# The first two steps of a recurrent attention and PReLU network, cut into named pieces and put in a new order

## The chip, the cores and the metric

The kernel runs on one core of a Trainium2 chip. The metric is the device time of one execution in microseconds; lower is better. The core's engines are TensorE (PE; PEld is its weight load), VectorE (DVE), ScalarE (ACT), GpSimd (POOL) and SyncE (SP). They run side by side, each takes its own instructions strictly in the order in which the program put them, and semaphores make one wait for another.

## What is computed

```python
# q, k, v, f_logit: (batch 4, heads 8, seq 768, head_dim 48), all float32
f = 1 / (1 + exp(-f_logit))
for t in range(S):
    state = f[:, :, t, :, None] * state + einsum('bhd,bhe->bhde', k[:, :, t], v[:, :, t])
    y[:, :, t] = einsum('bhd,bhde->bhe', q[:, :, t], state)
x = y.transpose(0, 2, 1, 3).reshape(3072, 384)      # tokens x (heads * head_dim)
h = x @ w_in                                        # 384 -> 2048
g = maximum(h, 0) + alpha * minimum(h, 0)
out = g @ w_out                                     # 2048 -> 384
```

A gated linear recurrence (a state of 48x48 per head that decays by f and takes in an outer product of k and v at each token), and behind it a network of two layers on each token.

## The kernel before

**Steps.** The sequence is cut into 6 chunks of 128 tokens, the batch into 2 pairs. A step is one chunk of one pair: 12 steps, `(bp, c)`, the pair changing fastest. So steps 0 and 1 are the first chunks of both pairs (c = 0), which have no state before them and take a form of their own for part of the work.

**Layout.** Head dimension lies on partitions, two heads in one tile (rows 0 to 47 and 64 to 111). A chunk has halves of 64 tokens (`CH`) and blocks of 32 (`DB`), a block 8 groups of 4 (`NB`).

**A step's stages** are Python generators; each `yield` ends a piece:

- `prepare` (P): loads of f, q, k and v (L266, L276; SyncE's queue in step 0, GpSimd's else). ScalarE makes the sigmoid and copies q to `qd` (L279, L282); VectorE makes products of neighbouring gates (`kr`) and queries lagged by 1 to 3 tokens (L287). Then two scans that give products of gates from a half's start and to its end (`ps`, `ss`, L317, L319), the query times its gate (`q4` within `us`, L321), the key times gates up to its group's end (`k4`, L347), and from these factors for groups further apart (`near`, L344, for c = 0; `earlier`, L330, else), keys carried to a block's or a half's end (`kh`, `ks`, `ended`, L374, L398), queries from a half's start (`q3`, `started`, L368, L406). For c = 0 it makes `k16` and `q16` (L387, L404), the two sides of the products between the two 16-token halves of a block. Last, ScalarE copies q3 into the matrix `A` (L419).
- `carry` (O): `across` (L476) makes the scores between the two blocks of a half and, for c = 0, the half-block products one block at a time (L486: 64 products of 32x16, both into the tile `off`), from where ScalarE copies them to `ad` (L490) and `A` (L494). For c = 0 `ks` is turned on TensorE (`pk`, L507) and copied to `ksn` (L510). `increments` (L460) makes the state's increments `pd`, `moved` (L443 to L449) the new state, kept in rows of `vs`.
- `attend` (S): for each of the two batches u, the scores of tokens up to 3 apart (`raw`, L532: k against the lagged queries), put where they belong by four masked copies (L538, `ad`), then the scores of groups further apart (`qu`, L548: k4 against us) with masked copies of their own (L570 for c = 0, L554 else). `ad` is copied into `A` (L576), `py` is A times `vs` (L587): 64 columns of values and state at once, and the step's output y is copied out (L596). In step 0 the tokens' layout for the network, `xT`, is made by products with a constant `dense` (L605) and copied (L607); in other steps by DMA (L616).
- `network` (n): 8 pieces `ph` (L631, x times w_in, two tiles of 128 features each), for each of which ScalarE makes `neg` (L636) and VectorE two `gate` (L638). Then the second product. Step 0 does it in full (`po`, L651); the other steps use 7 products of half size instead of 8 (`pa` to `pe`, L670, with sums of VectorE at L674 and L715).

**Weights.** They come in 8 pieces each for w_in and w_out: a load by SyncE and two conversions by ScalarE (L220 to L225; pieces `a` for w_in, `b` for w_out), and an add by VectorE (L234; pieces `w` and `v`). A load's buffer (5 of them) is free when ScalarE has converted it. `W` makes sums of quarters of w_out (L734).

**Order.** TensorE, VectorE and ScalarE take their instructions exactly in the order that `ORDER` gives; GpSimd's and SyncE's are put in order by what they wait for. `FIRST` lists the pieces around steps 0 to 3, `USUAL` all steps behind:

```python
FIRST = (
        "P5 a2 P a O w S w a w a2 S Q S O S w Q2 S Q2 S w",
        "a2 w2 n O b w n b2 S P v2 n2 S b v Q n b n O S2 v n b v n Q2 b v Q b n S v2 W Q W S n2 W n",
```

A letter stands for the next piece of that stage, a number for how often, `Q` for `P` of the step behind. The loop at the end calls `next(...)` on each.

**PSUM.** 8 banks: two pairs (`pair`: raw, qu, off, pk, pd, py take turns in two slots of two banks) and four single banks (`bank`: xt, ph, po, pa to pe). Before the first piece TensorE runs 56 tiny products (`IDLE`, L749).

Of the kernel before, what the change touches and what calls it, by code (L numbers as in the profile page):

```python
# [17 lines left out]
C = 128  # L18
# [12 lines left out]
FIRST = (  # L31
        "P5 a2 P a O w S w a w a2 S Q S O S w Q2 S Q2 S w",
        "a2 w2 n O b w n b2 S P v2 n2 S b v Q n b n O S2 v n b v n Q2 b v Q b n S v2 W Q W S n2 W n",
        "n S P n2 S W n W n Q n3 O S Q n S Q n Q S2 Q n3",
        "S n3 P S Q S n2 O n4 Q S Q S Q n S Q n Q n2",
# [3 lines left out]
def flat(first, usual, steps=12):  # L39
    out = []  # L40
    left = {}
    for n in range(steps + 1):
        for key in (first[n] if n < len(first) else usual).split():
            for _ in range(int(key[1:] or 1)):
                k = key[0]
                if k in "awbvW":
                    out.append((k,))
                else:
                    m = n - 1 if k == "n" else n + 1 if k == "Q" else n
                    k = "P" if k == "Q" else k  # L50
                    if 0 <= m < steps:
                        out.append((k, m))
    return out

ORDER = flat(FIRST, USUAL)


@with_exitstack
def kernel(
# [198 lines left out]
    def prepare(bp, c, x):  # L258
# [5 lines left out]
        def load(name, src, bufs=2):  # L264
            t = work.tile([128, W], F32, tag=name, name=f"{name}_{i}", bufs=bufs)
            loads.dma_start(out=t.rearrange("p (u x) -> p u x", u=U),  # L266
                              in_=src[b0:b0 + U, c].rearrange("u p h t -> p u (h t)"))
            return t

        f = quads(load("f", fT, 1))  # L270
        q = load("q", qT, 1)
        k = x["k"] = load("k", kT, 1)

# [4 lines left out]

        nc.scalar.activation(f, f, AF.Sigmoid)  # L279
        nc.scalar.copy(kr[:, :, 2:3], f[:, :, 3:4])  # L280
        qdv = [qd[:, :, QO[d]:QO[d] + NB * (4 - d)].rearrange("p g (i r) -> p g i r", r=4 - d) for d in range(4)]
        nc.scalar.copy(qd[:, :, 0:DB], q.rearrange("p (g t) -> p g t", t=DB))  # L282
        fq = fs[:, 0:NS - 1].rearrange("p (g i) -> p g i", i=NB + 1)[:, :, 1:NB + 1]
# [12 lines left out]
        yield  # L296

        ps = work.tile([128, NS], F32, tag="ps", name=f"ps_{i}", bufs=1)  # L300
        ut = work.tile([128, G * UW], F32, tag="us", name=f"us_{i}", bufs=1)
        if c:
            us = ut.rearrange("p (g t) -> p g t", g=G)
        else:

            at = (0, VW, VW + 16, VW + 16 + DB, VW + 16 + DB + NB)
            us, q16, k16, g16 = (ut[:, G * lo:G * hi].rearrange("p (g t) -> p g t", g=G) for lo, hi in zip(at, at[1:]))
            nc.gpsimd.memset(k16[:, :, 16:DB], 0.0)
            nc.gpsimd.memset(g16[:, :, 3:5], 1.0)
            x["q16"], x["k16"] = q16, k16  # L310
        x["us"] = us
        q4 = us[:, :, 0:DB].rearrange("p g (i r) -> p g i r", r=4)
        for r in range(4):
            nc.scalar.copy(q4[:, :, :, r], qdv[r][:, :, :, 0])
        if not c:
            nc.scalar.copy(g16[:, :, 2:6:3], fq[:, :, 3:5])
# [3 lines left out]
        yield  # L320
        nc.vector.tensor_tensor(q4, q4, f[:, :, 0:1].rearrange("p (g i) o -> p g i o", i=NB)  # L321
                                .broadcast_to((128, G, NB, 4)), ALU.mult)
        pre = ps[:, 0:NS - 1].rearrange("p (g i) -> p g i", i=NB + 1)
        suf = ss[:, 1:NS].rearrange("p (g i) -> p g i", i=NB + 1)[:, :, 1:NB + 1]

        def earlier(m):

            n = NB - m
            skip = UO[m - 1] + (8 if m == 2 else 4)
            nc.vector.tensor_tensor(  # L330
                us[:, :, UO[m]:UO[m] + 4 * n].rearrange("p g (i r) -> p g i r", r=4),
                us[:, :, skip:skip + 4 * n].rearrange("p g (i r) -> p g i r", r=4),
                fq[:, :, 1:1 + n].unsqueeze(3).broadcast_to((128, G, n, 4)), ALU.mult)

        def near(m, half=None):

            if m == 2:
                to, of = (us[:, :, o:o + 8].rearrange("p g (i r) -> p g i r", r=4) for o in (VO[2] + 8 * half, 16 * half + 8))
                by = fq[:, :, NQ * half + 1:NQ * half + 3]
            else:  # L340
                to = us[:, :, VO[3]:VO[3] + 8].rearrange("p g (i r) -> p g i r", r=4)
                of = us[:, :, VO[2]:VO[2] + 16].rearrange("p g (h r) -> p g h r", r=8)[:, :, :, 4:8]
                by = fq[:, :, 1:NB:NQ]
            nc.vector.tensor_tensor(to, of, by.unsqueeze(3).broadcast_to((128, G, 2, 4)), ALU.mult)  # L344

        k4 = x["k4"] = work.tile([128, W], F32, tag="k4", name=f"k4_{i}", bufs=1)
        nc.vector.tensor_tensor(k4, k, kr.rearrange("p n r -> p (n r)"), ALU.mult)  # L347
        if c:
            earlier(2)
        else:  # L350
            nc.vector.tensor_tensor(g16[:, :, 1:7:5], g16[:, :, 2:6:3], fq[:, :, 2:6:3], ALU.mult)
            near(2, 0)
            nc.vector.tensor_tensor(g16[:, :, 0:8:7], g16[:, :, 1:7:5], fq[:, :, 1:7:5], ALU.mult)
        yield


        q3 = x["q3"] = work.tile([128, GC, 3, DB], F32, tag="q3", name=f"q3_{i}", bufs=1)
        ks = x["ks"] = work.tile([128, GC, 2, DB], F32, tag="ks", name=f"ks_{i}", bufs=1)
        kh = x["kh"] = work.tile([128, GC, DB], F32, tag="kh", name=f"kh_{i}", bufs=1)
        f32 = pre[:, :, NB:NB + 1]  # L360

        some = slice(0, GC) if c else slice(1, GC, 2)

        def started(j):
            gs_ = some if j == 0 else slice(0, GC)
            js = slice(2 * (gs_.start or 0) + j, G, 2 * (gs_.step or 1))
            to = q3[:, gs_, 2 * j]
            nc.vector.tensor_tensor(to.rearrange("p g (i r) -> p g i r", r=4), q4[:, js],  # L368
                                    pre[:, js, 0:NB].unsqueeze(3).broadcast_to((128, to.shape[1], NB, 4)), ALU.mult)

        def ended(j):
            js = slice(j, G, 2)
            kj = ks[:, :, 1] if j else kh
            nc.vector.tensor_tensor(kj.rearrange("p g (i r) -> p g i r", r=4),  # L374
                                    k4.rearrange("p (g i r) -> p g i r", i=NB, r=4)[:, js],
                                    suf[:, js].unsqueeze(3).broadcast_to((128, GC, NB, 4)), ALU.mult)

        ended(0)
        if c:
            earlier(3)  # L380
        else:
            near(2, 1)
        ended(1)
        if c:
            earlier(4)
        else:
            nc.vector.tensor_tensor(k16[:, :, 0:16].rearrange("p g (i r) -> p g i r", r=4),  # L387
                                    k4.rearrange("p (g i r) -> p g i r", i=NB, r=4)[:, :, 0:NQ],
                                    g16[:, :, 0:NQ].unsqueeze(3).broadcast_to((128, G, NQ, 4)), ALU.mult)
        started(1)  # L390
        if c:
            earlier(5)
        else:
            near(3)
        yield
        if c:
            earlier(6)
        nc.vector.tensor_tensor(ks[:, :, 0], kh, f32[:, 1:G:2].broadcast_to((128, GC, DB)), ALU.mult)  # L398
        if c:
            kt = x["kt"] = late["kt"].tile([128, W], F32, tag="kt", name=f"kt_{i}")  # L400
            nc.vector.transpose(kt, ks.rearrange("p g s t -> p (g s t)"))
            earlier(7)
        else:
            nc.vector.tensor_tensor(q16.rearrange("p g (i r) -> p g i r", r=4), q4[:, :, NQ:NB], g16[:, :, NQ:NB].unsqueeze(3).broadcast_to((128, G, NQ, 4)), ALU.mult)  # L404
        by = f32[:, 2 * some.start:G:2 * (some.step or 1)]
        nc.vector.tensor_tensor(q3[:, some, 1], q3[:, some, 2], by.broadcast_to((128, by.shape[1], DB)), ALU.mult)  # L406
        started(0)

        f64 = x["f64"] = work.tile([128, U, H], F32, tag="f64", name=f"f64_{i}")
        by64 = pre.rearrange("p (a c j) i -> p a c j i", c=NC2, j=2)  # L410
        for cc in range(0 if c else 1, NC2 if c < NC - 1 else 1):
            for par in range(2):
                g64 = by64[rows(par), :, cc, :, NB]
                nc.vector.tensor_tensor(f64[halves(cc)[1], :, par:H:2].rearrange("p u h -> p (u h)"),
                                        g64[:, :, 0], g64[:, :, 1], ALU.mult)
        yield
        for cc in range(0 if c else 1, NC2):
            for par in range(2):
                nc.scalar.copy(A[halves(cc)[1], :, par * HP:(par + 1) * HP, CH * cc:CH * (cc + 1)],  # L419
                               q3[rows(par)].rearrange("p (u h c) s t -> p u h c (s t)", h=HP, c=NC2)[:, :, :, cc, 0:CH])  # L420
# [391 lines left out]
```

## Time and profile before

| what | value |
|---|---|
| time, median of 3 runs | 615.39 us (615.17 to 615.62) |
| the profiled execution's own time | 614.73 us |
| its span, from first to last instruction | 612.9 us |
| PE busy | 585.0 us (95%), 8220 instructions |
| PEld busy | 525.4 us (86%) |
| DVE busy | 496.7 us (81%), 997 instructions |
| ACT busy | 246.5 us (40%), 466 instructions |
| POOL busy | 62.8 us (10%) |
| mean granted TensorE clock | 0.997 |

How to read it: an engine's busy time is a sum over stages with different limits. The slices of the span, 40 of equal length, show where an engine is full: a digit is the busy share in tenths. The chain of waits names who waited for whom. The timeline has one row for instructions of one line that follow each other, with the idle time before the row in square brackets and what ended it; "issue" is a wait for nothing that the profile shows. A product in float32 leaves two records on PE, so a row's count is twice the number of instructions (not for the turns `pk`).

### The profile page before, as it was taken

The page shows a single profiled execution, that of the slowest core. Times are in us where ns is not written, and L with a number is a line of the kernel's source. Part 1 is how long each engine was busy: PE and PEld are TensorE (multiplying, and loading weights), DVE is VectorE, ACT ScalarE, POOL GpSimd, SP SyncE. Part 2 cuts the span into 40 slices and gives each one's busy share as a digit, 9 for nine tenths or more (in the row PEclk, how much of TensorE's full clock was granted, in tenths as well). Part 3 has the DMA queues.
Part 4 walks back from the last instruction along what each step waited for, and adds up shares of the span by engine and source line. Part 5 has one row for each costly group of instructions (what it writes and reads, how often), then busy time and mean ns, then how long its engine had stood idle before and what let it go on. Part 6 is the DMA issues. An engine that isn't in the chain of part 4 may idle for free.

```text
span 612.9 us, 19072 instructions
## 1 busy us (share of the span) xinstructions
PE 585.0 (95%) x8220; PEld 525.4 (86%) x8220; DVE 496.7 (81%) x997; ACT 246.5 (40%) x466; POOL 62.8 (10%) x117
## 2 busy tenths in 40 slices
PE   4569999999999999999999999999999999999997
PEld 3458867898899899899899899899899889889997
DVE  7599898899899798798798798798898889762251
ACT  5678852351641261272261261362252253232110
POOL 9120010001010011001001001001001000000000
PEclk9999999999999999999999999999999999999999
DMA  8966432104404214314313313313313401201000
GB/s 303 364 227 202 159 87 53 47 28 108 101 18 88 71 39 107 66 37 98 77 35 91 85 36 90 86 36 87 88 36 87 84 7 27 54 2 27 27 0 27
DMA packets 68116, 50.43 MB, mean 82 GB/s; under 512 B 47168, under 2 KB 60608, under 8 KB 68032
## 3 DMA queue, kind: packets, MB, share of 16 engines
q1 hardware_dynamic: 56656, 25.01, 15.7%
q0 software_dynamic: 6864, 22.35, 12.6%
q10 hardware_dynamic: 4512, 1.85, 1.7%
q8 instruction: 65, 1.06, 0.7%
q14 instruction: 19, 0.16, 0.1%
HBM read 36.21 MB, written 4.72 MB: 67 GB/s over the span
## 4 chain that ended last, share of the span: by engine, by line
PE 86%; DVE 9%; ACT 2%; issue 1%; DMA 1%; SPq 0%; ACTq 0%; DVEq 0%
PE ph L631 39%; PE pc L670 9%; PE pa L670 9%; PE pd L670 5%; PE pe L670 4%; PE pb L670 4%; PE py L587 3%; PE po L651 3%; PE raw L532 3%; PE qu L548 3%; PE pd L460 1%; PE off L476 1%; DVE ad L538 1%; DVE qd L287 1%; DVE gate L638 1%
## 5 line engine op out<-in xcount | busy, mean ns | idle before, releaser
L631 PE MATMUL ph<-xT,w_in_sb 128*128 128x256 f32 x1152 | 258.0, 382 | 1.4 <-DVE Csum L674 0.8
L631 PEld LDWEIGHTS ph<-xT,w_in_sb 128*128 128x128 f32 x1152 | 216.3, 190 | 34.0 <-issue 3.2
L636 ACT ACTIVATE neg<-ph 128x512 f32<-128x512 f32 x96 | 57.2, 596 | 189.1 <-PE ph L631 137.3
L638 DVE SCALAR_TENSOR_TENSOR gate<-neg,om,ph 128x256 f32<-128x256 f32 x192 | 82.7, 478 | 47.4 <-ACT neg L636 47.2
L670 PE MATMUL pc<-t,S 128*128 128x192 f32 x352 | 61.7, 329 | 0.0
L670 PE MATMUL pa<-w_out_sb,gate 128*128 128x192 f32 x352 | 61.4, 327 | 0.2 <-DVE gate L638 0.2
L670 PEld LDWEIGHTS pa<-w_out_sb,gate 128*128 128x128 f32 x352 | 57.9, 190 | 1.3 <-DVE gate L638 0.5
L670 PEld LDWEIGHTS pc<-t,S 128*128 128x128 f32 x352 | 57.3, 190 | 0.6
L538 DVE COPY_PREDICATED ad<-mraw,raw 128x256 f32<-128x256 int32 (+1 forms) x96 | 42.4, 442 | 10.7 <-PE raw L532 8.2
L554 DVE COPY_PREDICATED ad<-mquad,qu 128x224 f32<-128x224 int32 (+6 forms) x140 | 41.9, 299 | 6.2
L419 ACT COPY A<-q 48x512 f32<-48x512 f32 x44 | 27.2, 618 | 36.5 <-DVE q L368 36.1
L576 ACT COPY A<-ad 32x256 f32<-32x256 f32 x96 | 38.8, 404 | 1.4
L330 DVE TENSOR_TENSOR us<-us,fs 128x768 f32<-128x768 f32 (+5 forms) x60 | 36.8, 614 | 0.0
L691 ACT ACTIVATE o<-pa 128x192 f32<-128x192 f32 x11 | 3.6, 331 | 75.2 <-PE pa L670 72.3
L674 DVE SCALAR_TENSOR_TENSOR Csum<-pc,Csum 128x192 f32<-128x192 f32 x22 | 7.9, 357 | 29.6 <-PE pc L670 29.3
L715 DVE TENSOR_TENSOR S<-gate 128x512 f32<-128x512 f32 x44 | 30.3, 688 | 0.8
L532 PEld LDWEIGHTS raw<-qd,k 48*32 48x32 f32 x1536 | 18.6, 109 | 14.2 <-issue 12.0
L670 PE MATMUL pe<-w_out_sb,S 128*128 128x192 f32 x176 | 30.4, 326 | 0.0
L670 PE MATMUL pb<-t,gate 128*128 128x192 f32 x176 | 30.4, 326 | 0.0
L670 PE MATMUL pd<-w_out_sb,S 128*128 128x192 f32 x176 | 30.4, 326 | 0.0
L532 PE MATMUL raw<-qd,k 48*32 48x80 f32 x1536 | 24.1, 243 | 6.5 <-issue 3.4
L266 POOL DMA_DIRECT2D k<-in_kT x11 | 8.0, 728 | 207.4 <-PE raw L532 207.4
(101 smaller groups left out, 766.3 us busy)
## 6 DMA issues: line engine op xcount, KB each, us to landing
w_out_raw<-in_w_out SPq DMA_DIRECT2D x8, 767.8 KB, 5.8
w_in_raw<-in_w_in SPq DMA_DIRECT2D x8, 767.2 KB, 10.8
q<-in_qT POOLq DMA_DIRECT2D x11, 512.0 KB, 4.1
f<-in_fT POOLq DMA_DIRECT2D x11, 512.0 KB, 4.3
k<-in_kT POOLq DMA_DIRECT2D x11, 512.0 KB, 5.0
out<-o SPq DMA_DIRECT2D x24, 192.0 KB, 3.1
vs<-in_v POOLq DMA_DIRECT2D x22, 192.0 KB, 4.6
ksn<-kt SPq DMA_DIRECT2D x80, 32.0 KB, 2.0
```

The lines of the kernel that those rows point to most:

```text
L330: nc.vector.tensor_tensor(us[:, :, UO[m]:UO[m] + 4 * n].rearrange("p g (i r) -> p g i r", r=4), us[:, :, skip:skip + 4 * n].rearrange("p g ...
L419: nc.scalar.copy(A[halves(cc)[1], :, par * HP:(par + 1) * HP, CH * cc:CH * (cc + 1)], q3[rows(par)].rearrange("p (u h c) s t -> p u h c (s ...
L532: nc.tensor.matmul(raw[DB * j:DB * (j + 1), par, hp * C:hp * C + QW], lhsT=k[r_, g * DB:(g + 1) * DB], rhs=qd[r_, g], start=True, stop=True)
L538: nc.vector.copy_predicated(adu[:, :, :, d:4], mraw[:, d, :, d:4].bitcast(I32).unsqueeze(1).broadcast_to((128, H, NB, n)), rv[:, :, QO[d]: ...
L548: nc.tensor.matmul(qu[DB * j:DB * (j + 1), par, hp * QS + 4:hp * QS + QL], lhsT=k4[r_, g * DB:(g + 1) * DB], rhs=us[r_, g, 4:QL], start=Tr ...
L554: nc.vector.copy_predicated(ad[:, u, :, :, 4 * m:DB], mquad[:, lo:lo + n].bitcast(I32).unsqueeze(1).unsqueeze(1).broadcast_to((128, 2, HP, ...
L576: nc.scalar.copy(A[s_, u, :, s_], ad[s_, u].rearrange("p r h t -> p (r h) t"))
L631: nc.tensor.matmul(ph[:, j * T:(j + 1) * T], lhsT=w_in_sb[:, kt, m * 128:(m + 1) * 128], rhs=xT[:, kt], start=(kt == 0 and j == 0), stop=( ...
L636: nc.scalar.activation(neg, phv, AF.Relu, scale=-1.0)
L638: nc.vector.scalar_tensor_tensor(gate[:, m % NH, m // NH], neg[:, j], om[:, m:m + 1], phv[:, j], ALU.mult, ALU.add)
L670: nc.tensor.matmul(to[:, 0:DH], lhsT=of(f), rhs=by(f), start=(f == 0 and not more), stop=(f == NH - 1), skip_group_check=True)
L715: nc.vector.tensor_tensor(to, x_, y_, op)
```

## The change

Steps 0 and 1 (c = 0) are no longer run by the three generators. `opening` gives each of their parts a key of its own, a plain function, and `HEAD` lists the parts of both steps, the weight pieces and the network's pieces one by one. A leading 0 or 1 is the step; in the other words the number behind the letter is the step. `prepare`, `carry` and `attend` keep only the form for c > 0; the shared parts are moved into functions (`loaded`, `scanned`, `gated`, `keyed`, `started`, `ended`, `carried`, `begun`, `turned`, `increments`, `moved`, `across`, `crossed`, `scored`, `scored4`, `lags`, `placed`, `summed`, `by_token`) with the same instructions. `USUAL`, the network and the weight pieces are as before.

Within the two steps: `raw` (r) stands directly behind the lagged queries and takes both slots of the pair; the four `q3`, `kh` and `ks` products come before the group factors; the half-block products are made for four blocks at once (L626 there: a product of 128 keys with 64 queries, of which the diagonal squares of 32x16 are used) into the free end of `qu`, and copied out in four pieces of 16 partitions for each batch; in step 0 `off` and `pk` use single banks; `py`, the copy of y and the dense product are pieces by batch (`y`, `Y`, `x`).

```diff
-FIRST = (
-        "P5 a2 P a O w S w a w a2 S Q S O S w Q2 S Q2 S w",
...
+HEAD = (
+        "0f 0r0 0g a 0h 0i 0r1 0m 0j 0o a 0O 0l 0k 0p a 0R0 0K0 0q 0K1 0s 0u0 b 0t 0U0 0u1 0H0 0d 0R1 0U1 1f 0A0 0H1 "
+        "w 0D 0y0 0A1 0y1 0Y0 0Y1 w 0M 0x0 w 0x1 ",
+        "1r1 1g 1h 1r0 0X a 1i w 1j 1R0 a 1R1 w v a n0 b a w n0 1m a 1l n0 v w n0 w b n0 b 1p 1o v 1q b n0 1k 1O n0 b "
+        "v 1K0 1s 1K1 ",
+        "n0 1u1 1u0 n0 1U0 b v 1U1 P2 1H0 1A0 v 1d n0 1H1 b 1t 1D v 1y0 1A1 1y1 v W 1Y0 P2 1Y1 W 1X W W n0 1M P2 P2 "
+        "P2 n0 n1 S2 P2 W n1 n1 n1 n1 ",
+        "S2 S2 P3 n1 P3 n1 n1 O2 P3 S2 n1 n1 S2 P3 P3 n1 S2 n1 n1 S3 n2 P3 n2 S3 n2 n2 P4 n2 S3 S3 n2 O3 n2 n2 S3 S3 "
+        "P4 n2 P4 n2 P4 P4 n2 P4 n2 n2 ",
+)
...
+        def two(name):
+            if bp:
+                t = pair(name)
+                return t[:, 0], t[:, 1]
+            return bank(f"{name}a"), bank(f"{name}b")
...
+        def quads_of_half():
+            g16 = x["g16"]
+            nc.vector.tensor_tensor(g16[:, :, 1:7:5], g16[:, :, 2:6:3], fq[:, :, 2:6:3], ALU.mult)
+            near(2, 0)
+            nc.vector.tensor_tensor(g16[:, :, 0:8:7], g16[:, :, 1:7:5], fq[:, :, 1:7:5], ALU.mult)
+            near(2, 1)
+            near(3)
...
+        def quad_(u):
+            qu = x["qu", u] = pair(f"qu{u}_{i}")
+            scored4(qu, u, x, VW, C)
+            for hp in range(HP):
+                g = (u * HP + hp) * NJ
+                for par in range(2):
+                    r_ = rows(par)
+                    nc.tensor.matmul(qu[:, par, hp * C + 64:(hp + 1) * C], lhsT=x["k16"][r_, g:g + NJ].rearrange("p j t -> p (j t)"),
+                                     rhs=x["q16"][r_, g:g + NJ].rearrange("p j t -> p (j t)"), start=True, stop=True)
+
+        def halved(u):
+            qv = x["qu", u].rearrange("p r (h x) -> p r h x", h=HP)
+            for j in range(NJ):
+                s_ = slice(DB * j, DB * j + 16)
+                nc.scalar.copy(ad[s_, u, :, :, 16:DB], qv[s_, :, :, 64 + 16 * j:80 + 16 * j])
...
+        def out_(u):
+            if not u:
+                x["py"] = pair(f"py_{i}")
+            summed(x["py"], bp, u)
+
+        def kept_out(u):
+            if not u:
+                x["y"] = work.tile([128, U, HP, C], F32, tag="ksn", name=f"y_{i}", bufs=1)
+            nc.scalar.copy(x["y"][:, u].rearrange("p h t -> p (h t)"), x["py"][:, u])
+
+        def dense_(u):
+            if not u:
+                x["xt"] = [bank(f"xt{kt}_{i}") for kt in range(NK)]
+            for kt in range(NK):
+                pairs = [hp for hp in range(HP) if 2 * D * hp < 128 * (kt + 1) and 2 * D * (hp + 1) > 128 * kt]
+                for hp in pairs:
+                    o = 2 * D - 2 * D * hp + 128 * kt
+                    nc.tensor.matmul(x["xt"][kt][:, u * C:(u + 1) * C], lhsT=dense[:, o:o + 128], rhs=x["y"][:, u, hp],
+                                     start=(hp == pairs[0]), stop=(hp == pairs[-1]))
...
+        parts = {
+            "f": lambda: loaded(bp, c, x), "g": lambda: scanned(bp, c, x), "h": lambda: gated(bp, c, x),
+            "i": lambda: keyed(bp, c, x), "j": lambda: ended(0, x), "l": keys, "m": lambda: started(1, x),
+            "p": quads_of_half, "q": halves_of_block, "s": lambda: begun(bp, c, x), "t": lambda: turned(c, x),
+            "o": off_, "O": lambda: crossed(x["off"]), "k": turn, "d": lambda: increments(bp, c, x),
+            "D": lambda: moved(bp, c, x, 0), "M": lambda: moved(bp, c, x, 1), "X": given,
+        }
+        for key, part in (("r", raw_), ("R", lambda u: lags(x["raw", u], u)), ("u", quad_), ("H", halved),
+                          ("U", quartered), ("K", kept_keys), ("A", placed), ("y", out_), ("Y", kept_out), ("x", dense_)):
+            for u in range(U):
+                parts[f"{key}{u}"] = lambda part=part, u=u: part(u)
...
+        for key, n in ORDER:
+            part = pieces[key] if n is None else run[key, n]
+            part() if callable(part) else next(part)
```

`keys` (l) is `ended(1)` and `carried`; `raw_` and `off_` call `scored` and `across`, `turn` makes `pk`, `given` (X) copies the dense products to `xT` in step 0 and starts the DMAs of `by_token` in step 1. `quartered` (U) holds the three masked copies of L570.

## The prediction

> **What bounds the kernel now.** First the page's slices (15.3 us each):
>
> ```profile
> PE   4569999999999999999999999999999999999997
> DVE  7599898899899798798798798798898889762251
> ```
>
> TensorE fills every slice but the first three and the last; VectorE is nearly full until slice 34. So nearly all that can be saved is TensorE's empty time in the opening. Who it waits for there, from the chain of waits over the first 130 us (us in total, times, longest):
>
> ```profile
> PE off L476 <- DVE q L368: 9.5, 1, 9.5
> PE raw L532 <- issue: 3.4, 3, 2.0
> ...
> PE xt L605 <- ACT y L596: 2.0, 1, 2.0
> PE raw L532 <- ACT A L494: 1.8, 1, 1.8
> ...
> PE raw L532 <- DVE ad L538: 1.3, 1, 1.3
> PE pd L460 <- issue: 1.3, 1, 1.3
> ```
>
> Then the timeline of TensorE (start, us, tile, xcount of records, idle before):
>
> ```profile
> 17.70 1.08 PE L476 MATMUL off<-q,kh 48*32 48x32 f32 x64 [9.46 <-DVE q L368]
> ...
> 24.42 1.02 PE L532 MATMUL raw<-qd,k 48*32 48x80 f32 x38 [1.75 <-ACT A L494]
> ...
> 32.32 0.64 PE L532 MATMUL raw<-qd,k 48*32 48x80 f32 x22 [1.99 <-issue]
> ...
> 38.21 3.17 PE L587 MATMUL py<-A,vs 128*64 128x64 f32 x60 [0.64 <-ACT vs L449]
> 43.39 4.51 PE L605 MATMUL xt<-y,dense 128*128 128x256 f32 x12 [2.00 <-ACT y L596]
> 47.74 2.76 PE L631 MATMUL ph<-xT,w_in_sb 128*128 128x256 f32 x12
> ...
> 51.03 1.34 PE L486 MATMUL off<-us 48*32 48x16 f32 x128
> 52.52 1.09 PE L507 MATMUL pk<-ident,ks 128*128 128x128 f32 x8
> ```
>
> The network of step 0 (`ph`) starts at 47.74 us, and from there TensorE works almost without a wait to 612.9: 565.2 us. So the sum is: when does `ph` start, and what does TensorE still have to do then.
>
> A second reading: TensorE runs at half speed in the opening. 38 records of `raw` take 1.02 us (27 ns each) at 24.42, but 64 take 0.92 us at 63.70 (14 ns); the 12 of `xt` take 4.51 us, the 12 of `ph` behind them, of the same shape, 2.76. PEclk's 9s do not show it.
>
> **The change, part by part.** Times are from the span's start.
>
> 1. First scores. `raw0` and `raw1` need only qd and k. The last lagged query ends at 10.54 on VectorE, k landed at 7.8. Cold, each is 64 x 27 ns = 1.72 us: 10.6 to 14.1, in time in which TensorE now waits (9.46 us before `off`). Cost nothing; if that cover were gone, 3.4 us.
>
> 2. VectorE up to k4 is unchanged (starts at 12.95, the next at 14.11). Then four of 128x512 at a 0.60 us pitch (one q3, both ended, carried) to 16.5; five short ones of quads_of_half (0.20+0.33+0.19+0.33+0.33) to 17.9; the four lags of `raw0` (27.30 to 29.28: 1.98) to 19.9, where they stand at 27.3 now; two half-block factors (1.2) to 21.1; begun (0.33+0.34+0.36) to 22.1.
>
> 3. TensorE: `off` at 15.4 (needs kh and q3 only) for 1.08; `pk` to 18.6; `qu0` at 20.0, when lags of `raw0` free its PSUM pair: 64 records at 19 ns (58 in 1.10 at 26.89) and the 8 half-block products after 21.1, to 22.7.
>
> Those products: 128 records of 32x16, 1.34 us a step, become 16 instructions 128 wide and 64 long. Below by py's rows (64 columns, 32 instructions in 2.08: 65 ns): 1.0 us; above by pk's (128x128, 8 in 1.09: 136 ns): 2.2. I take 1.0, since like py they fill two tiles side by side: -0.3 a step.
>
> 4. Copies of those halves go from 2 to 8 a step, as 16-partition pieces of 128 elements. The row before is 0.43 us for 2 of the same length, so 0.8 us for four. They now stand on the path: after quartered(0) (1.00 us, to 23.7) ScalarE copies to 24.5; only that frees the pair that `qu1` takes (the built program has `qu1` wait for ScalarE). `qu1` 24.6 to 27.1, quartered(1) to 28.3, its copies to 29.2.
>
> 5. `pd` 27.1 to 29.0 (1.95), its copies to 30.0 (0.96); `py` to 33.8 (0.48+3.17). "Output by batch" does less than it says: in the built program the first copy of y waits for the last product of both batches. So y is 34.0 to 35.1 (1.07), and only the dense product starts after its first half, 34.6.
>
> 6. `xt` has the columns of before: 2.7 us at full speed, 5.3 at half. ScalarE has step 1's us copies between (2.17+0.32, to 37.6), hidden by it. Then both `raw` of step 1 (1.7 to 3.4) before `ph`. At half speed throughout, `ph` starts at 34.6+5.3+3.4 = 43.2; at full speed from `py` on (`py` then ends at 32.1), at about 37.1. In the trace `py`'s 60 records take 53 ns each, between the 32 of the `py` at 81.92 (64 in 2.08) and twice that, so the clock came up within it, and `xt`, behind a wait of 2.00, is slow again. The new order has no wait over 1 us from `pd` on, so I take 39.8.
>
> [...]
> [...] The rows show `pk` starting at 52.52 right behind 32-wide products that run to 52.37; so I price no drain.
>
> 7. What runs behind `ph`: the two `raw` (0.85 each at full speed) are done: -1.7.
>
> 8. "Issue" waits (0.96, 1.99, 1.30): time in which TensorE waits for nothing shown. They may come back at other places: 0 to 4.3. Some will fall into the waits before `qu0` and `qu1`: +1.5.
>
> 9. VectorE in the first network. From 28.3: step 1's lagged queries 3.65, two w_in adds 1.9, vs 2.0, w_in 1.0, scans, gate and k4 3.6, then a wait for ScalarE's conversion of w_in3, which stands behind xT, to 42; that add, kh, eight lags of step 1 (3.9), two adds: the first gate at about 49.3, ended 50.1. Four `ph` banks fill from 39.8 to 50.6 (2.69 each), so the fifth `ph` has 0.5 us of cover. If it is gone, each us late costs a us. +0.2.
>
> 10. Loads. SP's w_out0 goes ahead of w_in3, and w_in7's load waits until ScalarE converts w_in3 (40): landed 46 to 47, added at about 58, needed at 60 or later: cover 2 us. POOL issues q, f and k of step 1 at once (now k at 33.4).
>
> 11. Steps 2 and 3 have their pieces in another order, with no instruction added. TensorE is full there now (its waits behind 130 us in the profile, `ph` for Csum 0.8 and for issue 0.6, are small), which hides an earlier or later VectorE or DMA step; priced at nothing, 1 us more if a piece comes late.
>
> Sum: -7.9 (39.8 for 47.7) -1.7 -0.3 +1.5 +0.2 = -8.2. On the profiled execution, 614.73 (span 612.9 and 1.8 around it), that is 606.5; the median, 615.39, is 0.66 higher, so the forecast is 607.2. Best ends: -10.6-1.7-0.3+1.0 = -11.6, 603.8. Worst: -4.5-1.7+0.9 (`ph` still cold)+0.5 (products)+4.3 +1.0 = +0.5, 615.9.
>
> **Rivals.**
> A. The clock comes up early and issue waits hide: `ph` at 37.1, about 604. For: few waits from 24.6 on. Against: at 24.4 to 28.0 `raw` and `qu` at 70% duty stayed slow.
> B. VectorE becomes the bound of the first network: gates late by 3 to 6 us, cover 0.5: 610 to 613. For: VectorE is busy 19.7 of the 20 us from 40 to 60 now, and it sheds only the wait of 6.1 and 1.1 at `ad`, where TensorE wants 8. Against: its list above fits.
> C. Slower: ScalarE's queue. Step 1's sigmoid now stands before the copies of A, the second half-block copies, pd's and y. It is reached at 24.5 and needs f's load. In the trace that load was issued by POOL at 15.2 and landed at 23.6 (8.4 us; the median of such loads is 4.3), among weight loads that land every 2.03 us. Each us past 24.5 is a us on the path, and past 32.7 the gain is used up. Six weight loads served first would be 16.9+6x2.03 = 29.1, then q and f; at 35 the time is 617.7. Against: POOL's loads shared the engines with SP's.
>
> **How the numbers follow.** Forecast (605 to 610) 0.53, A 0.16, B 0.18, C 0.10, nothing left (within 0.2%) 0.03. A time within 0.2%, 1.2 us, can't be told from no change. Faster: 0.53+0.16+0.16 of B = 0.85; same 0.04; slower 0.11. The range goes from A to B: 603 to 612.5.
>
> **What would show it.** `raw` at 10.6 and `off` at 15.4; `qu0` near 20, `qu1` near 24.6 behind ScalarE's ad copies; `ph` at 37 to 43; no wait of `ph` for gates over 1 us. It is wrong if sigmoid waits for its DMA past 26, if `ph` waits for `gate`, or if TensorE shows new issue waits over 4 us before `ph`.

## The result, and the profile after

The changed kernel takes 606.56 us (median of 4 runs, 606.23 to 606.95), the kernel before 615.50 beside it: ratio 0.9855, 95% interval 0.9838 to 0.9873. The forecast was 607.2. The profiled execution took 606.23 us, its span is 604.5, so 8.4 us are gone from the span of 612.9.

The slices of the page (tenths busy, 15.1 us each):

```profile
PE   5689999999999999999999999999999999999997
DVE  7799999998898888889889899798798798761351
```

TensorE gains in the first three slices (4, 5 and 6 tenths before) and nowhere else that a tenth shows. Its chain of waits over the whole run (us in total, times, longest):

```profile
PE raw L489 <- DVE qd L289: 2.6, 1, 2.6
PE qu L498 <- ACT ad L633: 2.2, 1, 2.2
...
PE off_0a L463 <- DVE kh L358: 1.7, 1, 1.7
...
PE ph L716 <- issue: 0.9, 1, 0.9
...
PE raw L489 <- issue: 0.8, 2, 0.4
```

The one wait of 9.5 for q is now 2.6 + 1.7 with the first scores between them, and `raw`'s issue waits fell from 3.4 to 0.8. A new one, of `qu` for ScalarE's copies, is 2.2. The timeline of TensorE (start, us, tile, records, idle before):

```profile
10.88 2.12 PE L489 MATMUL raw<-qd,k 48*32 48x80 f32 x111 [2.64 <-DVE qd L289]
13.40 0.60 PE L489 MATMUL raw<-qd,k 48*32 48x80 f32 x17 [0.40 <-issue]
...
20.49 1.05 PE L498 MATMUL qu<-us,k 48*32 48x52 f32 x64 [1.54 <-DVE ad L506]
21.60 1.97 PE L626 MATMUL qu<-us 48*128 48x64 f32 x16
25.81 1.06 PE L498 MATMUL qu<-us,k 48*32 48x52 f32 x64 [2.23 <-ACT ad L633]
...
28.70 1.53 PE L436 MATMUL pd<-vs,ksn 64*48 64x48 f32 x64
31.18 0.48 PE L521 MATMUL py<-A,vs 128*64 128x64 f32 x4 [0.95 <-ACT ad L633]
...
36.02 2.92 PE L683 MATMUL xt<-y,dense 128*128 128x128 f32 x24 [0.78 <-ACT y L674]
...
40.65 0.47 PE L489 MATMUL raw<-qd,k 48*32 48x80 f32 x21 [0.38 <-issue]
41.05 13.22 PE L716 MATMUL ph<-xT,w_in_sb 128*128 128x256 f32 x60
```

`ph` starts at 41.05 for 47.74: 6.69 us earlier. Behind it stand 604.5 - 41.05 = 563.45 us for 565.2: 1.75 less. Together that is the 8.4. `xt` took 2.92 us, so TensorE's clock was up before it: the record of the granted clock has it at full from 34.66.

One line each from ScalarE's and VectorE's timelines, for the two queues that the rivals named:

```profile
25.78 1.06 ACT L283 ACTIVATE f<-f 128x1024 f32<-128x1024 f32 x1
```

```profile
49.29 0.86 DVE L723 SCALAR_TENSOR_TENSOR gate<-neg,om,ph 128x256 f32<-128x256 f32 x2
```

Step 1's sigmoid ran without a wait (f had landed at 24.26), and the first gate is at 49.29, as forecast, with no wait of `ph` behind it.

### The profile page after: what moved, and what is told of

The parts are those of the page before. It is cut to its first block, busy times and chain, and to the rows that moved or that the text cites. A ratio compares the mean times of both kernels' runs of the same rounds, so it can differ in the third digit from the quotient of the medians.

```text
span 604.5 us, 18724 instructions
## 1 busy us (share of the span) xinstructions
PE 585.7 (97%) x8040; PEld 526.9 (87%) x8040; DVE 495.7 (82%) x997; ACT 249.5 (41%) x478; POOL 62.8 (10%) x117
## 3 DMA queue, kind: packets, MB, share of 16 engines
q0 software_dynamic: 6864, 22.35, 13.1%
q8 instruction: 64, 1.05, 0.8%
## 4 chain that ended last, share of the span: by engine, by line
PE 90%; DVE 4%; ACT 2%; DMA 2%; SPq 1%; issue 1%; DVEq 0%; ACTq 0%
PE ph L716 40%; PE pc L755 9%; PE pa L755 9%; PE pb L755 5%; PE pe L755 4%; PE pd L755 4%; PE py L521 4%; PE po L736 4%; PE qu L498 3%; PE raw L489 3%; PE pd L436 2%; PE off L463 1%; SPq L422 1%; DMA ksn<-kt 1%; DMA f<-in_fT 1%
## 5 line engine op out<-in xcount | busy, mean ns | idle before, releaser
L325 ACT COPY us<-qd 128x256 f32<-128x256 f32 x48 | 27.0, 672 | 7.4 <-DVE qd L289 4.4
L289 DVE TENSOR_TENSOR qd<-qd,f 128x768 f32<-128x768 f32 (+2 forms) x36 | 27.1, 752 | 3.2 <-ACT qd L285 3.2
L498 PE MATMUL qu<-us,k 48*32 48x112 f32 (+1 forms) x1536 | 26.1, 259 | 3.8 <-ACT ad L633 2.2
```

What stands on the lines that cost most here:

```text
L289: nc.vector.tensor_tensor(qdv[d], qdv[d - 1][:, :, :, 1:5 - d], f[:, :, 1:5 - d].rearrange("p (g i) r -> p g i r", i=NB), ALU.mult)
L498: nc.tensor.matmul(qu[DB * j:DB * (j + 1), par, hp * QS + 4:hp * QS + QL], lhsT=x["k4"][r_, g * DB:(g + 1) * DB], rhs=x["us"][r_, g, 4:QL] ...
```

## The experiments

All times are medians, with the lowest and highest run; the ratio is to the kernel before on the same chip. The sizes of the waits are from one profiled execution each.

**Scores late.** The two first `raw` go back behind `pk`.

```diff
-"0f 0r0 0g a 0h 0i 0r1 0m 0j 0o a 0O 0l 0k 0p a 0R0 ...
+"0f 0g a 0h 0i 0m 0j 0o a 0O 0l 0k 0r0 0r1 0p a 0R0 ...
```

> Undoes the first part in step 0: both raw stand behind off and pk instead of in front of off. If the early first scores are what moves the path: raw can start at 18.9 when pk ends, 64 records take 1.2 us at the 19 ns of the changed kernel, so raw0's masked copies start at 20.2 instead of 18.3, qu0 at 22.2 instead of 20.5, and ph 1.7 us later than 41.05: 608.3 us against 606.6, or 607.6 if the clock still comes up at 34.7 and shortens xt. If the place of the scores does not matter and ScalarE's queue sets ph anyway: 606.6 to 606.9.

610.85 us (609.87 to 611.95), ratio 0.9932 (0.9915 to 0.9949): half of the gain is gone. `qu0` came at 22.35, as forecast, but then TensorE stood still twice more, for nothing that the profile names:

```profile
18.63 2.41 PE L489 MATMUL raw<-qd,k 48*32 48x80 f32 x128
22.35 0.80 PE L498 MATMUL qu<-us,k 48*32 48x52 f32 x38 [1.31 <-ACT w_out_sb L231]
24.97 0.58 PE L498 MATMUL qu<-us,k 48*32 48x52 f32 x26 [1.82 <-issue]
...
34.58 1.52 PE L436 MATMUL pd<-vs,ksn 64*48 64x48 f32 x60 [1.60 <-issue]
...
41.39 4.92 PE L683 MATMUL xt<-y,dense 128*128 128x128 f32 x24 [0.78 <-ACT y L674]
```

So the place of the scores is worth 4.3 us by the medians, more than the TensorE time that it hides (2.41 us here). This execution is the slowest of the four, and its `ph` starts at 47.77, 6.72 us later than in the changed kernel: `qu0` is 1.86 later and the two waits follow, and 2.0 us more come from `xt`, which takes 4.92 us for 2.92. The granted clock rises only at 45.59 here.

**One block at a time.** The half-block products again 32 wide and 16 long, 64 a step instead of 16; everything else is the changed kernel.

```diff
-                    nc.tensor.matmul(qu[:, par, hp * C + 64:(hp + 1) * C], lhsT=x["k16"][r_, g:g + NJ].rearrange("p j t -> p (j t)"),
-                                     rhs=x["q16"][r_, g:g + NJ].rearrange("p j t -> p (j t)"), start=True, stop=True)
+                for j in range(NJ):
...
+                        nc.tensor.matmul(qu[DB * j:DB * (j + 1), par, o:o + 16], lhsT=x["k16"][r_, g],
+                                         rhs=x["q16"][r_, g], start=True, stop=True)
```

> Undoes the second part alone, in both steps: the half-block products one block at a time again (32 of 32x16 for each batch instead of 8 of 128x64), into the same places of qu, with the same copies. If the four-at-once product costs TensorE time: step 1 gives back 2 x (1.03 - 0.67) = 0.7 us at full speed, step 0 2 x (1.97 - 0.72) = 2.5 us at half speed, all on the path: 603.4 us, and 604.5 if a wait takes up half of step 0's part. If the product is hidden (the rival, by which the prediction had it at -0.3 a step): 606.6 to 607.2.

A miss: 612.37 us (611.87 to 613.37), ratio 0.9961 (0.9948 to 0.9974). Its timeline:

```profile
21.51 0.83 PE L628 MATMUL qu<-us 48*32 48x16 f32 x64
...
28.22 0.50 PE L498 MATMUL qu<-us,k 48*32 48x52 f32 x22 [2.63 <-issue]
...
34.51 0.88 PE L436 MATMUL pd<-vs,ksn 64*48 64x48 f32 x28 [4.09 <-issue]
```

The products did what was expected: 0.83 us a batch for 1.97. But issue waits came, of 2.63, 4.09 and, at 71.97, 2.33 us. Behind the third the granted clock is at half for 3.41 us (73.02 to 76.44), so a part of the 5.8 us by which this kernel is slower than the changed one is the clock's. Nine microseconds of standing still that no semaphore explains became the question of the rest of the study.

**A new theory.** TensorE's instructions come by DMA, and they can come too late: that is the author's reading of the numbers that follow. The page's part on DMA queues has, for the changed kernel,

```profile
q8 instruction: 64, 1.05, 0.8%
```

64 packets of 16 KB; TensorE has 16,338 records in the trace (PE, PEld and its sequencer), so there is a packet for every 255 of them (in the kernel before 65 packets for 16,692, one for every 257). When these records are counted from the first, each of the issue waits of 0.3 us or more in `raw`, `qu` and step 0's `pd` but one stands at a number of the form 193 + 256 n. Such a number is called a border below:

| kernel | record number: wait (us) |
|---|---|
| before | 705: 0.96; 961: 1.99; 1985: 0.45 |
| changed | 449: 0.40; 1473: 0.38 |
| scores late | 705: 1.82; 961: 1.60 |
| one block at a time | 961: 2.63; 1217: 4.09; 2497: 2.33 |
| pair freed early (below) | 961: 0.45 |

The exception is the 1.30 of `pd` in the kernel before, at 1144, and it is a wait for VectorE. A semaphore instruction of TensorE lasts from 33.53 to 35.16 there, and the last of these four masked copies of `raw1` ends at 35.11:

```profile
33.24 1.88 DVE L538 COPY_PREDICATED ad<-mraw,raw 128x256 f32<-128x256 int32 x4 [1.11 <-PE raw L532]
```

From the moment at which TensorE crosses one border to the moment at which it goes on behind the next after a wait, there are 6.63 and 5.92 us in the kernel before (449 to 705, 705 to 961), 5.77 with late scores, 6.29 at the second wait of one block at a time, all while the DMA engines are full (from 20 to 32 us a share of 1.03 to 1.05 in the kernel before); and 3.79 us at its third wait, where they are idle. TensorE runs through as many records of 48x32 products faster than that: of a batch's `qu` and half-block products, one block at a time, 256 records take 1.28 us at full clock (67.33 to 68.61). The DMA view of that kernel from 24 to 36 us, and from 66 to 72:

```profile
DMA  9999999999999999999999999999999973222202
...
q8 instruction: 3, 0.05, 1.7%
```

```profile
DMA  0000000000000000000000000300000000000000
...
q8 instruction: 1, 0.02, 1.0%
```

In the first every slice of DMA is full until 33.6 us, with two instruction packets among the loads (from 25.43 and 31.90) and a third behind them (35.71); in the second the one packet is the only traffic, and TensorE waits for it until 71.97.

**Opening products.** If that is so, work that costs nothing moves the waits. The 56 tiny products at 2 to 8 us are 4 records each. Eight fewer move every border 32 records on in the program, eight more 32 back.

```diff
-IDLE = 56
+IDLE = 48    # the other kernel: 64
```

> The changed kernel with 48 instead of 56 of the tiny products that open TensorE's program (they run at 2 to 8 us, ahead of everything on the path; nothing else differs, and no result depends on them). Theory (TensorE's instructions arrive in packets of 256 records, and the next packet needs 4 to 6 us from the moment the one before it is begun): eight products are 32 records, so every packet border lies 32 records later in the program. Borders then fall at the old records 481 (end of the first scores), 737 (inside qu0) and 1505 (raw of step 1): the issue waits of 0.40 and 0.38 us at the old records 449 and 1473 go, waits of 1 to 2.5 us come at 737 and 1505, ph starts at 42.5 to 45 us instead of 41.05, and the time is 608.0 to 611.0. Rival (the waits belong to the products at which they stand: a drain, a dependence): waits at the same products as before, ph within 0.3 us of 41.05, time 605.8 to 607.2.

> The changed kernel with 64 instead of 56 of the tiny opening products, the same edit in the other direction. Theory (packets): borders lie 32 records earlier, at the old records 417, 673, 929, 1185 and 1441; none of them is reached faster than 4 to 6 us behind the one before, so no issue wait over 0.3 us is left before ph and the time is 605.2 to 606.6, no longer than the changed kernel's although TensorE has eight products more. Rival (an effect of the opening products themselves, on the clock or on what follows them): the time moves against that of 48 products by the same small step on both sides of 56, or not at all.

With 48: 609.78 us (609.18 to 611.93), ratio 0.9918 (0.9892 to 0.9944). With 64: 604.94 us (603.79 to 606.13), ratio 0.9833 (0.9807 to 0.9859). The first is as the theory of packets had it; the second a little under its range, and it had excluded the wait of 0.67 that came. Both directions from 56 differ by 4.8 us, with less work giving the longer time. With 48:

```profile
16.87 0.34 PE L489 MATMUL raw<-qd,k 48*32 48x80 f32 x1 [3.77 <-issue]
...
23.07 0.41 PE L498 MATMUL qu<-us,k 48*32 48x52 f32 x10 [1.78 <-issue]
...
33.13 1.20 PE L436 MATMUL pd<-vs,ksn 64*48 64x48 f32 x44 [1.90 <-issue]
```

These are records 449, 705 and 961 again, in other products than before: the last one of `raw1`, ten from the end of `qu0`'s 64, and within `pd`. `ph` starts at 46.24, beyond the 45 that was expected, the wait in `pd` was not expected, and the one at 1473 did not come. This execution is the slowest of the four (611.93), and its `xt` takes 5.17 us for 2.92: the granted clock rises only at 44.35. With 64:

```profile
13.21 0.87 PE L489 MATMUL raw<-qd,k 48*32 48x80 f32 x33 [0.67 <-issue]
15.52 0.26 PE L463 MATMUL off_0a<-q,kh 48*32 48x32 f32 x1 [1.44 <-DVE kh L358]
...
36.23 4.84 PE L683 MATMUL xt<-y,dense 128*128 128x128 f32 x24 [0.78 <-ACT y L674]
```

The wait at 449 has 1.44 us of slack behind it, and no later issue wait is listed in this run: those of `ph` (0.9) and `off` (0.5) in the changed kernel are gone too. So this kernel is the faster one although its `xt` ran at half the granted clock for most of its time (4.84 us for 2.92; the clock rises at 40.3) and its `ph` started 1.47 us later, at 42.52.

**One block at a time, borders moved.** The same shift for the kernel of the miss, `IDLE = 16`.

> The kernel with the half-block products one block at a time (612.37, with issue waits of 2.63, 4.09 and 2.33 us at its records 961, 1217 and 2497), now with 16 instead of 56 tiny opening products: packet borders lie 160 records later, at its old records 609, 865, 1121, 1377, 2401. Theory (packets): the three waits leave 961, 1217 and 2497 and new ones stand at 865, 1121 and 2401, of 0.5 to 2.5 us each; part of 865's lies in qu1's wait for ScalarE, so the sum before ph falls and ph starts at 41.5 to 44.0 instead of 44.65: 609.0 to 612.0. Rival (a drain at each change of tile shape): the waits stay where they were and the time stays within 612.0 to 613.0.

615.32 us (613.36 to 617.02), ratio 1.0005 (0.9987 to 1.0023). The waits moved exactly as the theory said, to its records 705, 961 and 2241 (the old 865, 1121 and 2401), but the sizes were missed: 4.48, 3.55 and 1.95 us, and 1.37 more at 449. The time is outside both ranges. Places follow from the count of records; sizes need the moment at which each packet comes, and the author's estimate of 4 to 6 us from border to border was too short: from 449 to 705 it was 8.64 us here, and with 48 opening products 10.06 from 705 to 961. What starts a packet no run here tests. The traces of all kernels have 67 crossings of a border before 40 us, and at 63 of them just one instruction packet comes between that border and the next, starting 0.1 to 7.5 us behind the crossing.

**The kernel before, borders moved.** Is the change's gain only a luckier place of borders? `IDLE = 48` and 64 in the kernel before.

> The kernel before with 48 instead of 56 opening products. How much of the change's 8.9 us is the order, and how much the place of the packet borders? Theory (the order's demand: raw, qu and raw want three packets in 10 us where 6 us each are needed, wherever the borders lie): issue waits again at TensorE's records 705 and 961, which are now other products of the program, 3 to 5.5 us together before ph; time 614.0 to 618.0. Rival (mostly the place of the borders): one of this and the kernel before with 64 opening products falls below 610.

> The kernel before with 64 instead of 56 opening products. Theory (order): issue waits at records 705 and 961 again, 2 to 4.5 us together before ph; 612.0 to 616.0. Rival (place of the borders): below 610.

619.43 us (618.04 to 620.30), ratio 1.0071 (1.0054 to 1.0088), and 615.99 (614.30 to 619.43), ratio 1.0011 (0.9990 to 1.0033). Both wait at records 705 and 961, 1.39 and 1.72 us with 48, 1.31 and 1.77 with 64. The first is above its range for a third wait, at 1729:

```profile
55.58 0.61 PE L486 MATMUL off<-us 48*32 48x16 f32 x38 [3.67 <-issue]
```

which stands in the half-block products one block at a time. The granted clock is at half there as well, from 53.64 to 60.47. With 48, 56 and 64 opening products the old order gives 619.4, 615.0 to 615.5 and 616.0, the new one 609.8, 606.6 and 604.9. No border tried brings the old order near 610, so the order is worth 8 to 11 us at each place; borders are worth up to 5 by themselves. `pd`'s wait of 1.3 us is there in all three kernels of the old order, on no border, and in all three it ends 0.1 us behind VectorE's last masked copy of `raw1` (34.82 for a `pd` at 34.92 with 48, 34.87 for 34.97 with 64).

**Output whole.** `y` as one, and `xt` in 6 products of 256 columns.

```diff
-"w 0D 0y0 0A1 0y1 0Y0 0Y1 w 0M 0x0 w 0x1 ",
+"w 0D 0A1 0y0 0y1 0Y0 0Y1 w 0M w 0x0 ",
...
-                    nc.tensor.matmul(x["xt"][kt][:, u * C:(u + 1) * C], lhsT=dense[:, o:o + 128], rhs=x["y"][:, u, hp],
+                    nc.tensor.matmul(x["xt"][kt][:, 0:T], lhsT=dense[:, o:o + 128], rhs=x["y"][:, :, hp],
```

> Undoes the third part in step 0: both halves of A placed, then py of both batches, both copies of y, then the dense products of both batches at once (6 of 256 columns). If the output by batch only lets the dense product start after the first copy: xt 0.5 us later, and half of py's start lost (A of the second batch is placed at 33.8, py could start at 31.2), together +0.5 to +1.5: 607.1 to 608.1 us. If it carried nothing: 606.6. If it were the main part of the gain: 609 or more.

607.54 us (606.35 to 608.55), ratio 0.9883 (0.9864 to 0.9901): within the forecast, 1.0 us over the changed kernel by the medians, with runs that overlap. `xt` waited 1.27 us for y instead of 0.78. The rest isn't separated: `xt` took 4.47 us for 2.92 in the profiled execution, and with six products fewer the borders behind it moved, so that no issue wait of 0.3 us is left. "Output by batch" is the small part that the built order said it would be.

Taken out one by one, the three parts cost 4.3, 5.8 and 1.0 us, more together than the 8.9 of the whole. Each also changes what meets the borders and when the clock rises, so they are no shares of it.

**Pair freed early.** The lags of `raw1` ahead, both `qu` in a row, so that `qu1` needn't wait for ScalarE; and the same with 64 opening products.

```diff
-... 0K1 0s 0u0 b 0t 0U0 0u1 0H0 0d 0R1 0U1 1f ...
+... 0K1 0R1 0s 0u0 0u1 b 0t 0U0 0H0 0d 0U1 1f ...
```

> Takes away the wait of 2.2 us of qu1 for ScalarE's copies: raw1's masked copies come ahead of begun, so raw1's pair is free before qu1 and both qu run in a row. If that wait is on the path by itself: ph 2 us earlier, 604.6 us. If ScalarE's queue takes its place (step 1's sigmoid and copies, A's copies, the second half-block copies, which py waits for): 606.2 to 606.8, with the idle time before py up from 0.9 to about 2.6 us.

> The lags of raw1 ahead and both qu in a row (606.01 with 56 opening products), with 64 opening products. Theory (packets): the border at record 961 is now met 32 records earlier in the program, inside qu1 or pd, and its wait of 0.5 to 1.8 us lies in py's wait of 2.9 for ScalarE; the later issue waits (ph 1.5, pd 0.5) go, so the time falls by 0.8 to 2.5 us: 603.5 to 605.2, the best so far or level with the kernel of 64 opening products (604.94). Rival (qu in a row asks for instructions faster than they come): an issue wait of over 2 us ahead of pd that shows in ph, 606 to 608.

606.01 us (605.01 to 607.92), ratio 0.9862 (0.9840 to 0.9884), 0.2 us under the range for ScalarE's queue, and 605.27 (603.53 to 606.02), ratio 0.9827 (0.9791 to 0.9863). `qu1` starts at 23.34 with no wait, 2.47 us earlier, and all of it comes back two stages on:

```profile
31.52 0.48 PE L521 MATMUL py<-A,vs 128*64 128x64 f32 x4 [2.91 <-ACT ad L633]
```

ScalarE's list, not the pair, sets `py`. With 64 opening products the wait at record 961 (1.70 us, in `qu1`) is hidden in that of `py`, as expected; the time is just above its range and level with 604.94.

**Sigmoid later.** Step 1's `loaded` part behind both `py`.

```diff
-... 0R1 0U1 1f 0A0 0H1 w 0D 0y0 0A1 0y1 0Y0 ...
+... 0R1 0U1 0A0 0H1 w 0D 0y0 0A1 0y1 1f 0Y0 ...
```

> The changed kernel with step 1's loaded part (its sigmoid, two copies on ScalarE, seven VectorE operations) moved from ahead of the copies of A of batch 0 to behind both py. Theory (the place is right because VectorE has only 0.5 us of cover at the first gate, and raw of step 1 needs the lagged queries): the issue order of ScalarE frees py by some 2.5 us, but raw of step 1 then waits about 2 us for qd, ph starts no earlier than 41, and the fifth ph waits 0.5 to 1.5 us for the first gate: 607.5 to 610.0. Rival (ScalarE's queue is what the path waits for between qu1 and y, so 2.8 us of step 1's work taken out of it come back at ph): ph at 38.5 to 39.5, 604.0 to 605.3.

609.58 us (608.66 to 610.29), ratio 0.9905 (0.9880 to 0.9930): the theory's range.

```profile
37.57 4.47 PE L683 MATMUL xt<-y,dense 128*128 128x128 f32 x24 [1.91 <-ACT y L674]
...
55.61 2.83 PE L716 MATMUL ph<-xT,w_in_sb 128*128 128x256 f32 x12 [0.95 <-ACT w_in_sb L231]
```

Not by the expected steps, though. `py` is freed no sooner (31.45); the sigmoid's time is met by `xt` (1.91 for y) and only 0.27 us are left at `raw`. `xt` then takes 4.47 us for 2.92, because the granted clock, up at 35.24, is at half again from 38.65 to 42.07, and `ph` starts at 44.03. VectorE's first gate slides to 54.61, and the fifth `ph` waits 0.95 us, which the profile puts down to ScalarE's conversion of w_in. But VectorE adds the piece of w_in then converted only from 55.39 to 56.43, behind this `ph`'s start, so that can't be what it needed; the gate, which ended at 55.46, is the likelier releaser.

**Filled.** `IDLE = 60`, and four wide products whose result is overwritten, in the waits ahead of `qu1` (two), `py` and `xt`.

```diff
-... 0t 0U0 0u1 ... 0D 0y0 ... 0M 0x0 ...
+... 0t 0U0 0z2 0u1 ... 0D 0z1 0y0 ... 0M 0z1 0x0 ...
+        def filled(n):
...
+            for _ in range(n):
+                nc.tensor.matmul(x["xt"][0][:, 0:256], lhsT=ident, rhs=ones[:, 0:256], start=True, stop=True)
```

> The changed kernel with 60 opening products and four added products of 128 columns of lhsT by 256 columns, whose result is overwritten: two ahead of qu1, one ahead of py, one ahead of xt, all in TensorE's waits there (2.23, 0.95 and 0.78 us; by the xt and ph rows some 0.9 us each at half speed, 0.45 at full). Theory (the granted clock rises at the end of a window of 3.4 us that TensorE filled, and it is the wide products that fill it): the clock is up before xt, which takes 2.7 to 3.0 us instead of 4.84 in the kernel with 64 opening products, ph starts at 40 to 41 instead of 42.52, time 602.5 to 604.3. Rival (the clock's rise depends on where its windows happen to lie, or the added products only push the path): ph at 42 to 44, time 604.5 to 607.0.

603.78 us (603.62 to 604.09), ratio 0.9806 (0.9769 to 0.9843), the fastest version of the study: 2.8 us under the changed kernel by the medians, with no run in common.

```profile
23.30 2.07 PE L690 MATMUL xt<-ones,ident 128*128 128x256 f32 x4
...
36.38 3.07 PE L683 MATMUL xt<-y,dense 128*128 128x128 f32 x24
...
40.90 13.22 PE L724 MATMUL ph<-xT,w_in_sb 128*128 128x256 f32 x60
```

`xt` took 3.07 us, `ph` started at 40.90, as the theory had it. Against 64 opening products (604.94) its gain is at the edge of the spread; that its four runs lie within 0.5 us, where the other's lie within 2.3, could come of a clock that is up before `xt` in each run and not in some, which isn't shown: the clock's rise was read in one execution of each. The two causes, borders and clock, were both changed from the changed kernel's, so how the 2.8 us split between them isn't separated.

## Why the prediction was right

The time was right to 0.6 us and the path was the one forecast. By the steps:

- **First scores (1).** 10.88 to 14.0, for 10.6 to 14.1, inside the wait. "Cost nothing" was too modest: taken out of that place they cost 4.3 us. `qu0` is 1.86 us later, issue waits of 1.82 and 1.60 us come at the borders 705 and 961, and in the execution that was profiled the clock rose at 45.59 instead of 34.66.
- **Off, pk, qu0 (2, 3).** 15.71, 18.95 and 20.49, for 15.4, 18.6 and 20.0.
- **Half-block products (3).** The failed term. They are 1.11 us a batch at full speed (64.48 and 66.27) and 1.97 at half: 2.2 us a step against 1.34, +0.9 where the sum had -0.3, at the upper bound that was named. Eight products a batch are 139 ns each, the price of pk's rows (136) and not of py's (65). The reason given for py's price, two tiles side by side, still fits: the records start in pairs 7 ns apart, as py's do. But a pair follows the next at 112 ns (64.64 and 64.75), py's at 58 (78.99 and 79.05). Their weights have 128 columns and py's 64; that this is the cause isn't shown. The part is worth 5.8 us all the same by the second experiment, not in TensorE's own time but by the issue waits that come without it, and the clock lost behind one of them: 48 fewer products a step are 192 of TensorE's records, which was no term at all.
- **Copies and qu1 (4).** `qu1` waited for ScalarE's `ad` copies, as named; they took 1.06 us for 0.8, and it started at 25.81 for 24.6.
- **pd, py, xt (5, 6).** 28.70, 31.18 and 36.02, 1.2 to 1.6 us behind the forecast; `y` ran 35.29 to 36.36. No wait from `pd` on was over 1 us (0.95, 0.50, 0.78), and `xt` ran at the full granted clock (2.92 us; at full from 34.66).
- **ph (6).** 41.05, within 37.1 to 43.2, for 39.8 taken. Behind it 1.75 us less, for the two `raw` priced at 1.7 (7), but that agreement is partly luck. From start to start `raw` does take 1.73 us less there. The half-block products take 0.74 more and issue waits 0.5 more, and waits for data fell from 1.4 to 0.4, in the order that was priced at nothing (11).
- **Issue waits (8).** +1.5 taken, 0.4 + 0.38 before `ph` found, where the kernel before has 0.96 + 1.99 (its 1.30 is a wait for VectorE); 1.4 more come later, in `ph` and `off` (1.1 in the kernel before). Their price between 0 and 4.3 was a guess about an unknown thing, and it hit by the accident of where the borders fell: with eight opening products fewer the same order would have given 609.8.
- **VectorE, loads, order of steps 2 and 3 (9 to 11).** The first gate at 49.29 for 49.3 and no `ph` wait behind it.

So -6.69 and -1.75 stand for the terms' -8.2: `ph` 1.25 later than taken and the products dearer, paid for by issue waits that came off lighter and by waits for data behind `ph` that went. Rival A's early clock came, at 34.7 us by the granted clock's record (the kernel before had lost it again from 44.3 to 47.7), but not its `ph` at 37, since waits for ScalarE stood ahead. Rival B's gates were not late, though the sigmoid moved later shows how little cover they have. Rival C's load landed 1.5 us ahead of its sigmoid.

A drain of TensorE where the tile shape changes was priced at nothing, and the records show a price. Behind 15 us the changed kernel has 105 places where the tile shape changes and nothing else is waited for, and at every one the next product starts 69 to 71 ns ahead of the modelled end of the one before. Between products of one shape it is 163 ns or more in 99 of 100. From `qu`'s 32-wide products to the half-block ones it is 136 ns from start to start (64.48), where one block at a time, with no change of shape, has 26 (67.97). So by the author's estimate, 136 less 26 ns, a change costs some 0.1 us, too little to move the forecast. The row that the prediction went by, `pk` at 52.52, starts 0.15 us behind the modelled end and so can't speak against a drain.

The granted clock's records turn at steps of 3.41 us: half from 44.32 to 47.74 in the kernel before, up at 35.24, half at 38.65 and up again at 42.07 with the sigmoid later, half from 73.02 to 76.44 one block at a time. The first rise, at 34.7, 36.8, 40.3 and 45.6 us in four kernels (changed, filled, 64 opening products, scores late), belongs to no one place in the work: it falls into the end of `py`, the start of `xt` and twice the end of `xt`. That a stretch filled with work is enough to raise it, as the theory of the filled kernel has it, these runs don't show: with the pair freed early TensorE ran without a wait from 20.32 to 26.63 us, with `qu`, half-block products and the first `pd`, and the clock rose only at 35.7. Where it fell, TensorE had waited for a part of the 3.41 us ahead: 2.00 us (the kernel before, at 44.32), 1.91 (sigmoid later, 38.65) and 2.33 (one block at a time, 73.02).

## What to carry to other kernels

Read "issue" in the chain of waits as a question: count the engine's instructions up to each such wait, and see whether the numbers repeat at a fixed distance. Here they did, at 256 records, and they stood at such numbers again with 32 records more or fewer at the start and with 160 fewer, so the author reads them as waits for the program and not for data. Three things that changed such waits here can be tried elsewhere: fewer and larger products (48 more of the short ones a step cost 5.8 us), short ones placed in stretches where the engine waits anyway (the first scores, 4.3 us), and a shift of the borders by some idle instructions (4.8 us between 48 and 64 opening products). A wait off that distance is another matter: `pd`'s 1.30 was a wait for a semaphore that the profile's list of waits had not named. A change that removes a wait should be weighed with both of its neighbours: here freeing `qu1` only moved the wait to `py`, and moving the sigmoid only moved it to `xt`.

## What the runs showed of the hardware

Instruction packets of 16 KB came while the program ran: 64 of them, the first at 10.95 and the last at 597.50 us, for TensorE's 16,338 records in the changed kernel, one for every 255, and the issue waits of 0.3 us or more in `raw`, `qu` and step 0's `pd` stood at record numbers 256 or a multiple of it apart (449 and 1473 there; 705, 961 and 1985 in the kernel before). Of the 22 waits of 0.3 us or more at a border before 40 us, in all kernels, 16 ended 5.6 to 6.8 us behind the crossing of the border ahead and six 7.4 to 10.1 us; with the DMA engines idle it was 3.8 and 3.5 us (at 71.97 and 75.48, one block at a time with 56 and 16 opening products). The packet itself starts in the trace 2.2 to 2.8 us before TensorE goes on. Eight tiny products at the start, 4 records each and off the path, moved the time by 3.2 us (48 against 56) and 1.6 us (64 against 56) in the same direction: more of them was faster.
